# Order of the weight and key/value transfers on SyncE in a fused retention and gated-MLP kernel

## Chip, cores and metric

The kernel runs on one core of one Trainium2 chip. The metric is the device time of one execution in microseconds (us); the figure for a kernel is the median of its runs.

## What is computed

The first half is a retention layer: per batch (4) and head (8), a 64x64 state decays by a fixed factor per head and gains an outer product of key and value at each of 768 positions; the query reads it. The second half is a two-layer network with an elementwise gate on the 3072 resulting rows of 512 numbers.

```python
for t in range(S):
    state = gamma[None, :, None, None] * state + np.einsum('bhd,bhe->bhde', k[:, :, t], v[:, :, t])
    y[:, :, t] = scale * np.einsum('bhd,bhde->bhe', q[:, :, t], state)
...
h = x @ w_in                      # 3072x512 by 512x2048
sp = np.maximum(h, 0.0) + np.log1p(np.exp(-np.abs(h)))
g = h * erf(sp)
return (g @ w_out).astype(np.float32)   # 3072x2048 by 2048x512
```

The weights `w_in` and `w_out` arrive as 64-bit numbers and are turned into 32-bit ones on the chip.

## The kernel before

**Tiling.** The 3072 rows are cut into 24 chunks of 128 positions and 12 groups of 256 rows (two chunks a group). The hidden width of 2048 is cut into 8 pieces of 256. Weight pieces are numbered 0 to 7 for `w_in` and 8 to 15 for `w_out`; a raw piece of `w_out` is 1 MB of 64-bit words in one of four buffers of the pool `wide`.

**Stages.** The first four chunks (groups 0 and 1) go through a start-up stage. Then the loop at L881 runs over groups 2 to 11, each in eight slots `i`. A slot emits `unit` (L598), the first product for one of the 8 hidden pieces: 24 matmuls on TensorE (L608), three terms of operands that are split into high and low parts. Its `put` (L625) joins the terms on ScalarE (L256) and VectorE (L257) and has GpSimd store the piece of hidden values to a scratch area (L631). When all groups are done, the hidden values are read back, gated and multiplied by `w_out` (L792).

**Retention inside the loop.** While group g multiplies, the two chunks 2g+2 and 2g+3 of the next group are computed between its units. `begin` (L483; scores L489, state updates L496) runs ahead of unit 2 in groups 4 to 9 (ahead of unit 3 in group 2, 2 in group 3); `results` (L518) ahead of unit 5. `begin` needs the values scaled by L473.

**Loads for the group after.** In group g, `load_pair(2g+4)` (L113) fetches the chunks that `begin` uses in group g+1. It is a generator that yields after every four transfers: eight batches of four 32 KB transfers for keys and queries in blocks (`kb`, `qb`, L122), then one last batch with keys and values of both chunks, 256 KB each, in the order kn, v, kn, v (L131, L111). I call these 36 transfers a pair. `steps(pair, 2)` at L889 advances the generator by two batches in each slot, so kn and v come in slot 4. `prepare` (L457) scales the queries and transposes the blocks in slot 7, and scales the values (L473) in slot 0 of the next group.

**Conversion of w_out.** `conversion` (L165) turns a raw piece into 32-bit numbers in five steps: L181 with L182 on ScalarE; L185; L189; L192, after which the raw buffer is free; L203. `convert` advances it by 1, 2, 1, 1 and 2 steps in slots 0 to 4 of groups 4 to 9, seven a group, in the lists that `beside` (L825) returns. So piece 8 starts in slot 0 of group 4, piece 14 in slot 1 of group 8 and piece 15 in slot 0 of group 9.

**Where raw pieces are asked for.** Piece 8 in slot 4 of group 2; pieces 9, 10 and 11 in slots 1, 3 and 5 of group 3; pieces 12 to 15 inside `conversion`, behind L192 of the piece four before (L197, L198), which falls in groups 4, 5, 5 and 6. All these transfers, and those of a pair, are issued by SyncE (queue SP).

**What sets the order.** The schedule is written by hand: each engine executes its instructions in the order in which the Python code emits them. A tile's buffer comes from its pool in the order in which buffers were given back, and the first writer waits for the last reader of the tile before. For SyncE the program also lets each transfer wait until the one eight issues earlier has landed, so eight at most are under way, and an instruction that waits holds back all behind it.

Of the kernel before, what the change touches and what calls it, by code (L numbers as in the profile page):

```python
# [40 lines left out]
def kernel(  # L41
# [22 lines left out]
    NPC = n_ft // 2  # L64
# [14 lines left out]
    def b4(name, shape, dtype=F32):  # L79
        return big.tile([P] + shape, dtype, name=name, tag="b4")  # L80
# [19 lines left out]
    def load(j):  # L100

        kq = b4("kq", [2, H, D])
        KN[j], QN[j] = kq[:, 0], kq[:, 1]
        for to, src in ((KN[j], k), (QN[j], q)):
            nc.sync.dma_start(to, of_chunk(src, j))

    def load_values(j):
        if j % 2 == 0:
            VP[j] = b4("v", [2, H, D])
        V[j] = VP[j - j % 2][:, j % 2]  # L110
        nc.sync.dma_start(V[j], of_chunk(v, j))  # L111
# [32 lines left out]
    def load_piece(n, *parts):  # L144

        if n not in RAW:
            RAW[n] = b8("raw", [2 * d_model], I64)
        if n < NPC:
            rows = (slice(2), slice(2, 4)) if n == 0 else (slice(4),)
            for part, g, r in itertools.product(parts or (None,), rows, range(2)):  # L150
                f = slice(2 * P) if part is None else slice(part * P, (part + 1) * P)
                nc.sync.dma_start(
                    RAW[n][r * D : (r + 1) * D].rearrange("p (g f) -> p g f", g=n_k)[:, g, f],
                    w_in[r * DH : (r + 1) * DH, n * 2 * P : (n + 1) * 2 * P].rearrange(
                        "(g p) f -> p g f", p=D
                    )[:, g, f],
                )
        else:
            i = n - NPC
            nc.sync.dma_start(  # L160
                RAW[n].rearrange("p (f c) -> p f c", f=2),
                w_out[i * 2 * P : (i + 1) * 2 * P, :].rearrange("(f p) c -> p f c", p=P),
            )

    def conversion(n):  # L165

        WF[n] = b4("w", [2, 2, 2 * P])
        POWER[n] = b4("power", [2, 2, 2 * P])  # L170
        parts = itertools.product(
            range(2) if n < 4 else (None,), (slice(1), slice(1, 2)) if n == 0 else (slice(None),)
        )
        for part, rows in parts:
            last = n > 0 or rows.start == 1
            f = slice(2 * P) if part is None else slice(part * P, (part + 1) * P)
            words = RAW[n].bitcast(U32).rearrange("p (h a b w) -> p h a b w", h=2, a=2, w=2)[:, rows, :, f]
            to, power = WF[n][:, rows, :, f], POWER[n][:, rows, :, f].bitcast(U32)
            number = to.bitcast(U32)
            lo, hi = words[..., 0], words[..., 1]  # L180
            nc.vector.tensor_scalar(power, hi, 0x7FF00000, None, op0=ALU.bitwise_and)  # L181
            nc.scalar.activation(power, power, AF.Relu, bias=below, scale=8.0)  # L182
            if part is None:
                yield
            nc.vector.tensor_scalar(  # L185
                number, hi, 0xFFFFF, 1 << 20, op0=ALU.bitwise_and, op1=ALU.bitwise_or
            )
            yield
            nc.vector.scalar_tensor_tensor(to, number, 2.0**32, lo, op0=ALU.mult, op1=ALU.add)  # L189
            if part is None:  # L190
                yield
            nc.vector.scalar_tensor_tensor(  # L192
                power, hi, 1 << 31, power, op0=ALU.bitwise_and, op1=ALU.bitwise_or
            )
            if part != 0 and last:
                del RAW[n]
                if n + 4 < NPC or n >= NPC and n + 4 < 2 * NPC:  # L197
                    load_piece(n + 4)  # L198
                if n < 2:
                    load(JPC + n)  # L200
                    load_values(JPC + n)
            yield
            nc.vector.scalar_tensor_tensor(  # L203
                to, to, 2.0**-52, power.bitcast(F32), op0=ALU.mult, op1=ALU.mult,
            )
            if last and n < NPC:
                done.update(("in", 2 * n + u) for u in (range(2) if part is None else (part,)))
            yield
        if n >= NPC:
            nc.gpsimd.dma_start(  # L210
                WOF[n - NPC], WF.pop(n).rearrange("p h a f -> p (h a f)").rearrange("p (f c) -> p f c", f=2)
            )
# [472 lines left out]
    def steps(s, n=1):  # L685
        for _ in range(n):
            next(s, None)

    pair = load_pair(JPC + 2)
    prep = prepare(JPC + 2)  # L690
    a, b = JPC, JPC + 1
# [120 lines left out]
    def on_pe(g):  # L812

        a, b = 2 * g + 2, 2 * g + 3
        if a >= NJ:
            return {}
        if g < NG - 2:
            m = 3 if g == G2 else 2
            return {
                m: [(begin, a, ps_h), (begin, b, ps_r)],  # L820
                5: [(results, a, None, ps_h), (results, b, None, ps_r)],
            }
        return {1: [(begin, a)], 2: [(results, a)], 3: [(begin, b)], 5: [(results, b)]}

    def beside(g, prep, next_prep):  # L825

        a, b = 2 * g + 2, 2 * g + 3
        if g == G2:
            return {
                1: [(split_weights, 4)],  # L830
                2: [(split_weights, 5)],
                3: [(states, a), (states, b)],
                4: [(split_weights, 6), (load_piece, 8)],
                5: [(crossed_sums, a), (split_x, a)],
                6: [(crossed_sums, b), (split_x, b)],
                7: [(steps, next_prep, 3)],
            }
        if g == G2 + 1:
            return {
                0: [(steps, prep)],  # L840
                1: [(split_weights, 7), (load_piece, 9)],
                2: [(states, a)],
                3: [(states, b), (load_piece, 10)],
                5: [(crossed_sums, a), (split_x, a), (load_piece, 11)],
                6: [(crossed_sums, b), (split_x, b)],
                7: [(steps, next_prep, 3)],
            }
        if g < NG - 2:
            return {
                0: [(steps, prep), (convert, 1)],  # L850
                1: [(convert, 2)],
                2: [(states, a), (convert, 1)],
                3: [(states, b), (convert, 1)],
                4: [(convert, 2)],
                5: [(crossed_sums, a), (split_x, a)],
                6: [(crossed_sums, b), (split_x, b)],
                7: [(steps, next_prep, 3)],
            }
        if g == NG - 2:
            return {  # L860
                0: [(steps, prep), (load_w_out, 0)],
                1: [(states, a), (load_w_out, 1)],
                2: [(crossed_sums, a), (split_w_out, 0), (load_hiddens, 0)],
                3: [(states, b), (split_x, a)],
                4: [(split_w_out, 1), (softplus, 0)],
                5: [(erf, 0), (crossed_sums, b), (load_w_out, 2)],
                6: [(split_x, b), (gated, 0), (load_hiddens, 1)],
                7: [(split_w_out, 2), (split_g, 0)],
            }
        return {  # L870
            0: [(split_g, 1), (softplus, 1), (load_w_out, 3)],
            1: [(erf, 1), (load_w_out, 4)],
            2: [(split_w_out, 3), (load_w_out, 5)],
            3: [(gated, 1), (split_w_out, 4)],
            4: [(split_g, 2), (load_w_out, 6), (load_hiddens, 2)],
            5: [(split_w_out, 5), (load_w_out, 7)],
            6: [(split_g, 3)],
            7: [(split_w_out, 6)],
        }

    for g in range(G2, NG):  # L881
        pair = load_pair(2 * g + 4) if 2 * g + 4 < NJ else iter(())
        next_prep = prepare(2 * g + 4) if 2 * g + 4 < NJ else iter(())
        pe, other = on_pe(g), beside(g, prep, next_prep)
        for i, n in enumerate((0, 7, 1, 2, 3, 4, 5, 6) if g == G2 else range(NPC)):
            for f, *args in pe.get(i, ()):
                f(*args)
            put = unit(g, n)
            steps(pair, 2)  # L889
            if g == NG - 1:  # L890
                W.pop(n)
            for f, *args in other.get(i, ()):
                f(*args)
            put()
        prep = next_prep
    split_w_out(7)

    for n in range(NG * NU):
        g, i = divmod(n, NU)
# [62 lines left out]
```

## Time and profile before

| what | value |
|---|---|
| runs | 641.16, 638.66 and 639.08 us, median 639.08 |
| profiled execution | 644.27 us, of which the span from first to last instruction is 642.6 us |
| TensorE matmul (PE) busy | 624.8 us, 97% of the span |
| VectorE (DVE) busy | 473.7 us, 74% |
| ScalarE (ACT) busy | 346.5 us, 54% |
| GpSimd (POOL) busy | 81.6 us, 13% |
| SyncE's queue of transfers (q1) | 75.92 MB, 48.8% of 16 DMA engines |
| GpSimd's queue (q0) | 29.38 MB, 12.6% |
| mean granted TensorE clock | 0.986 of full speed |

The profile is of one execution. Times in its rows are microseconds from the first instruction, except where ns is written. PE is the matmul stream of TensorE, DVE is VectorE, ACT ScalarE, POOL GpSimd, and SPq is SyncE's instruction stream, where a row's length is the time that issuing took, waits included. A row of the waits names who waited, for whom, the total in us, how often and the longest. L numbers are lines of the kernel before.

### The profile page before, as it was taken

What the parts mean: (1) busy time and instruction counts of PE and PEld (TensorE: products, weight loads), DVE (VectorE), ACT (ScalarE), POOL (GpSimd) and SP (SyncE); (2) the same over time, 40 slices, a digit from 0 to 9 for tenths busy, and PEclk for the clock granted to TensorE, in tenths of its full rate; (3) what the DMA queues carried; (4) which work ended last, traced back from release to release, by engine and by line L of the source; (5) the groups of instructions that cost most, each with busy time, mean ns of one, the idle gap of its engine ahead of it and who ended that gap; (6) DMA issues with size and microseconds to landing.
All of it is one profiled execution on the core that took longest, in us unless ns stands there. A gap on an engine that the chain in (4) does not pass through costs nothing.

```text
span 642.6 us, 14651 instructions
## 1 busy us (share of the span) xinstructions
PE 624.8 (97%) x6080; PEld 562.2 (87%) x6080; DVE 473.7 (74%) x618; ACT 346.5 (54%) x432; POOL 81.6 (13%) x157
## 2 busy tenths in 40 slices
PE   8999999997989997999999999999999999999997
PEld 7788899997989997999999988888888888888886
DVE  4988998754767876787776998776867686777650
ACT  3333443231413231323237877988898889888920
POOL 1054421110211211122111110000000000000000
PEclk9999999997989997999999999999999999999999
DMA  9999776878778986768865662534253325323300
GB/s 190 218 210 240 207 176 154 223 204 225 217 158 223 258 229 157 199 173 207 213 206 166 204 239 82 165 110 137 83 163 132 88 108 163 132 78 120 99 33 33
DMA packets 165042, 106.36 MB, mean 166 GB/s; under 512 B 139248, under 2 KB 143600, under 8 KB 164976
## 3 DMA queue, kind: packets, MB, share of 16 engines
q1 hardware_dynamic: 154784, 75.92, 48.8%
q0 software_dynamic: 9632, 29.38, 12.6%
q8 instruction: 47, 0.77, 0.5%
q10 hardware_dynamic: 560, 0.14, 0.1%
q14 instruction: 19, 0.16, 0.1%
HBM read 69.75 MB, written 35.65 MB: 164 GB/s over the span
## 4 chain that ended last, share of the span: by engine, by line
PE 61%; DMA 1%; SPq 1%; DVE 1%; issue 0%; ACT 0%; DVEq 0%
PE o L792 20%; PE o L608 16%; PE hp L792 10%; PE r L792 10%; DMA v<-in_v_dram 1%; PE hp L608 1%; PE r L608 1%; SPq L131 1%; PE hp L496 0%; PE r L534 0%; PE hp L489 0%; PE r L545 0%; PE r L489 0%; PE r L496 0%; PE hp L534 0%
## 5 line engine op out<-in xcount | busy, mean ns | idle before, releaser
L608 PE MATMUL o<-x_hi,w_hi 128*128 128x256 f32 x600 | 152.6, 291 | 0.0
L608 PE MATMUL o<-x_lo,w_lo 128*128 128x256 f32 x600 | 149.7, 286 | 0.0
L608 PEld LDWEIGHTS o<-x_hi,w_hi 128*128 128x128 f32 x600 | 117.4, 196 | 1.6
L608 PEld LDWEIGHTS o<-x_lo,w_lo 128*128 128x128 f32 x600 | 117.4, 196 | 0.1
L256 ACT ACTIVATE h<-o 128x512 f32<-128x512 f32 x75 | 44.2, 593 | 104.5 <-PE o L608 103.7
L747 DVE TENSOR_TENSOR e<-hid,e 128x1024 f32<-128x1024 f32 x48 | 56.7, 1222 | 58.2 <-ACT e L737 58.2
L608 PE MATMUL o<-x_dif,w_dif 128*128 128x256 f32 x600 | 84.1, 283 | 0.0
L608 PEld LDWEIGHTS o<-x_dif,w_dif 128*128 128x128 f32 x600 | 77.4, 192 | 0.0
L631 POOL DMA_DIRECT2D hid<-h x80 | 44.2, 552 | 243.6 <-DVE h L257 237.8
L792 PE MATMUL o<-w_dif,g_dif 128*128 128x512 f32 x192 | 73.7, 389 | 0.0
L257 DVE SCALAR_TENSOR_TENSOR h<-o,h 128x512 f32<-128x512 f32 x75 | 51.2, 683 | 29.8 <-ACT h L256 19.2
L792 PE MATMUL o<-w_hi,g_hi 128*128 128x512 f32 x168 | 65.4, 389 | 0.0
L792 PE MATMUL o<-w_lo,g_lo 128*128 128x512 f32 x168 | 65.4, 389 | 0.0
L250 DVE SCALAR_TENSOR_TENSOR g_dif<-g_hi,g_lo 128x1024 fp32r<-128x1024 f32 x48 | 58.8, 1225 | 3.2
L248 ACT ACTIVATE g_hi<-e 128x1024 fp32r<-128x1024 f32 x48 | 51.0, 1062 | 17.8 <-DVE e L747 15.1
L249 DVE TENSOR_TENSOR g_lo<-e,g_hi 128x1024 fp32r<-128x1024 f32 x48 | 58.6, 1222 | 0.2
L583 PE MATMUL hp<-xT,w 128*128 128x256 f32 x256 | 57.2, 382 | 1.4 <-ACT xT L447 1.3
L583 PEld LDWEIGHTS hp<-xT,w 128*128 128x128 f32 x256 | 48.0, 190 | 8.6 <-ACT xT L447 1.5
L182 ACT ACTIVATE power<-power,below 128x1024 uint32<-128x1024 uint32 (+2 forms) x22 | 20.2, 920 | 54.9 <-DVE power L181 52.4
L737 ACT ACTIVATE e<-e 128x1024 f32<-128x1024 f32 x48 | 48.2, 1053 | 0.3
L733 ACT ACTIVATE e<-hid 128x1024 f32<-128x1024 f32 x48 | 48.2, 1052 | 0.3
L792 PEld LDWEIGHTS o<-w_dif,g_dif 128*128 128x128 f32 x192 | 36.0, 188 | 7.4
(164 smaller groups left out, 1078.3 us busy)
## 6 DMA issues: line engine op xcount, KB each, us to landing
hid<-hid SPq DMA_DIRECT2D x48, 512.0 KB, 4.7
hid<-h POOLq DMA_DIRECT2D x80, 256.0 KB, 3.4
raw<-in_moe_w_out_dram SPq DMA_DIRECT2D x8, 1024.0 KB, 7.4
v<-in_v_dram SPq DMA_DIRECT2D x24, 256.0 KB, 5.4
out_dram<-y SPq DMA_DIRECT2D x23, 256.0 KB, 2.1
kb<-in_k_dram SPq DMA_DIRECT2D x144, 32.0 KB, 2.9
qb<-in_q_dram SPq DMA_DIRECT2D x144, 32.0 KB, 2.7
kn<-in_k_dram SPq DMA_DIRECT2D x18, 256.0 KB, 5.0
```

Source lines behind the costliest of these rows:

```text
L248: nc.scalar.activation(hi, x, AF.Copy, scale=KEEP)
L249: nc.vector.tensor_tensor(lo, x, hi.bitcast(F32), op=ALU.subtract)
L250: nc.vector.scalar_tensor_tensor(dif, hi.bitcast(F32), Z, lo.bitcast(F32), op0=ALU.mult, op1=ALU.subtract)
L256: nc.scalar.activation(to, a, AF.Copy, scale=1 + 1 / Z)
L257: nc.vector.scalar_tensor_tensor(to, b, -1 / Z, to, op0=ALU.mult, op1=ALU.add)
L583: nc.tensor.matmul(HP_[ft][:, g], w[:, kk, ft % 2 * P : (ft % 2 + 1) * P], XC[g][:, kk], start=(kk == 0), stop=(kk == n_k - 1),)
L608: nc.tensor.matmul(to[:, u], W[n][i][:, kk * 2 * P + u * P : kk * 2 * P + (u + 1) * P], X[g][i][:, kk], start=(u == 0 and kk == 0 and i == ...
L631: nc.gpsimd.dma_start(HID[g][:, 2 * n : 2 * n + 2], h)
L733: nc.scalar.activation(E[n], HID_[n], AF.Softplus)
L737: nc.scalar.activation(E[n], E[n], AF.Erf)
L747: nc.vector.tensor_tensor(E[n], HID_.pop(n), E[n], op=ALU.mult)
L792: nc.tensor.matmul(Y[g][t][x // 2], G[n][x][:, f, t * P : (t + 1) * P], W_OUT[ft // 2][x][:, ft % 2 * d_model : (ft % 2 + 1) * d_model], s ...
```

## The change

Three things change.

1. `conversion` no longer asks for a piece of `w_out`; only the pieces of `w_in` are still asked for there.
2. `beside` asks for the pieces instead: 9 and 10 in slots 3 and 5 of group 3 (9, 10 and 11 in slots 1, 3 and 5 before), and then one a group, piece g+7 in slot 3 of groups 4 to 8. The request stands behind the slot's `convert`.
3. `steps(pair, 3)` advances the pair by three batches a slot, so the batch with kn and v comes in slot 2, ahead of the request for the raw piece in slot 3.

```diff
             if part != 0 and last:
                 del RAW[n]
-                if n + 4 < NPC or n >= NPC and n + 4 < 2 * NPC:
+                if n + 4 < NPC:
                     load_piece(n + 4)
...
         if g == G2 + 1:
             return {
                 0: [(steps, prep)],
-                1: [(split_weights, 7), (load_piece, 9)],
+                1: [(split_weights, 7)],
                 2: [(states, a)],
-                3: [(states, b), (load_piece, 10)],
-                5: [(crossed_sums, a), (split_x, a), (load_piece, 11)],
+                3: [(states, b), (load_piece, 9)],
+                5: [(crossed_sums, a), (split_x, a), (load_piece, 10)],
...
-                3: [(states, b), (convert, 1)],
+                3: [(states, b), (convert, 1)] + [(load_piece, g + 7)] * (g + 7 < 2 * NPC),
...
             put = unit(g, n)
-            steps(pair, 2)
+            steps(pair, 3)
```

## Prediction

> **What bounds the kernel now.** First the slices of the page: TensorE is busy nearly everywhere, and its granted clock dips in slices 9, 11 and 15 (about 145 to 257 us).
>
> ```profile
> PE   8999999997989997999999999999999999999997
> PEclk9999999997989997999999999999999999999999
> ```
>
> Then the waits of the engines, for what TensorE lacks there.
>
> ```profile
> DVE v L473 <- DMA v<-in_v_dram: 15.9, 4, 6.5
> PE hp L496 <- DVE v L473: 9.6, 3, 4.0
> ```
>
> TensorE waits three times for the scaled values, VectorE four times for the values to land; TensorE has no other wait over 1.5 us. Then the chain of work that ended last shows how the third stall came about.
>
> ```profile
> 235.08 4.32 SPq L131
> 239.44 6.27 DMA v<-in_v_dram
> 245.80 1.24 DVE v L473
> 247.08 1.13 PE hp L496 x32
> ```
>
> SyncE was late in issuing kn and v; the values landed at 245.71, and TensorE went on 1.4 us after that. Last, the starts of the first `begin` matmul of groups 3 to 10 give the price, in the timeline of TensorE.
>
> ```profile
> 122.84 0.69 PE L489 MATMUL hp<-qT,kT 64*64 64x64 f32 x32
> 150.30 0.69 PE L489 MATMUL hp<-qT,kT 64*64 64x64 f32 x32
> 154.96 1.13 PE L496 MATMUL hp<-v,kn 64*64 64x64 f32 x32 [3.96 <-DVE v L473]
> 184.36 0.69 PE L489 MATMUL hp<-qT,kT 64*64 64x64 f32 x32
> 187.12 0.69 PE L496 MATMUL hp<-v,kn 64*64 64x64 f32 x32 [2.07 <-DVE v L473]
> 215.38 0.69 PE L489 MATMUL hp<-qT,kT 64*64 64x64 f32 x32
> 242.84 0.69 PE L489 MATMUL hp<-qT,kT 64*64 64x64 f32 x32
> 247.08 1.13 PE L496 MATMUL hp<-v,kn 64*64 64x64 f32 x32 [3.54 <-DVE v L473]
> 276.49 0.69 PE L489 MATMUL hp<-qT,kT 64*64 64x64 f32 x32
> 303.72 0.69 PE L489 MATMUL hp<-qT,kT 64*64 64x64 f32 x32
> 328.31 0.69 PE L489 MATMUL hp<-qT,kT 64*64 64x64 f32 x32
> ```
>
> An undisturbed group takes 27.46 us (122.84 to 150.30, 215.38 to 242.84) or 27.23 (276.49 to 303.72; groups 5 and 8, whose first chunk opens a batch). The disturbed ones take 34.06, 31.02 and 33.65, so they lose 6.60, 3.79 and 6.19: **16.6 us** together. The idle time is only 9.6 of that. The rest is clock: after a stall the matmuls run slower for some microseconds.
>
> ```profile
> 150.00:160.00 10.00, 6.04 (x126) 5.65 (x125) 4.52 (x6) 2.12 (x3) 0.54 (x1) 0.68 0.85 211
> 180.00:190.00 10.00, 7.93 (x168) 7.54 (x168) 7.07 (x9) 1.19 (x2) 1.08 (x2) 0.89 0.79 160
> ```
>
> In these stretches of the busy times (PE, PEld, DVE, ACT, POOL, then clock, DMA share, GB/s) the clock is 0.68 and 0.89. The Trainium skill ("TensorE: Matmul & The Clock Gate", section "Part 1: The HAM clock gate") has the clock halve after an idle window of about 3.4 us. The stalls of 3.96 and 3.54 agree; the one of 2.07 us lost 3.79, more than the rule lets it.
>
> **Why SyncE is late.** Its timeline from group 2 on: the first block transfers of each pair (kb), some of the raw pieces, and the last v of the pair that began at 241.01.
>
> ```profile
> 88.62 2.80 SPq L122 DMA_DIRECT2D kb<-in_k_dram  x4
> 112.55 1.08 SPq L160 DMA_DIRECT2D raw<-in_moe_w_out_dram  x1
> 113.73 2.82 SPq L122 DMA_DIRECT2D kb<-in_k_dram  x4
> 127.16 0.45 SPq L160 DMA_DIRECT2D raw<-in_moe_w_out_dram  x1
> 140.80 0.46 SPq L160 DMA_DIRECT2D raw<-in_moe_w_out_dram  x1
> 151.42 2.63 SPq L122 DMA_DIRECT2D kb<-in_k_dram  x4
> 182.49 2.56 SPq L122 DMA_DIRECT2D kb<-in_k_dram  x4
> 211.18 2.94 SPq L122 DMA_DIRECT2D kb<-in_k_dram  x4
> 233.50 0.40 SPq L160 DMA_DIRECT2D raw<-in_moe_w_out_dram  x1
> 241.01 4.00 SPq L122 DMA_DIRECT2D kb<-in_k_dram  x4
> 264.53 1.37 SPq L111 DMA_DIRECT2D v<-in_v_dram  x1
> 269.75 1.88 SPq L122 DMA_DIRECT2D kb<-in_k_dram  x4
> 290.96 4.33 SPq L122 DMA_DIRECT2D kb<-in_k_dram  x4
> ```
>
> A pair without raw pieces takes 23.9 us (88.62 to 112.55) or 21.2 (269.75 to 290.96). The four pairs from 113.73 to 241.01 take 127.28, with pieces 9 to 15 among them and the tail of piece 8. With a pair at 23.9 that is (127.28 - 95.6)/8 = 4.0 us for a raw piece, and 27.9 us for a pair with one piece; with 21.2 it is 5.3 and 26.5. Before, seven pieces stand ahead of the values of pair 16, the last that stall; so SyncE falls behind, although a pair with one piece would about fit a group of 27.4.
>
> **The change, part by part.**
>
> *Raw pieces.* No transfer is added or dropped. Pieces 9 and 10 go behind the values of pair 10, pieces 11 to 15 behind those of pairs 12 to 20. Ahead of pair 16's values stand only 9 to 12, three pieces fewer, 12 to 16 us of SyncE's time by the two prices: about what was lost by then.
>
> *Three batches a slot.* By itself this moves nothing: SyncE has its next instructions queued and works at transfers. It only sees to it that kn and v are emitted ahead of slot 3's piece. Two slots earlier kn and v take buffers given back at the last group's end, at nearly the same place in the order, so I cost that at 0. SyncE does wait for buffers:
>
> ```profile
> SPq L122 <- DMA raw<-in_moe_w_out_dram: 11.0, 5, 2.9
> SPq L122 <- PE o L608: 9.0, 6, 3.9
> ```
>
> The second row is buffers that TensorE frees; it keeps SyncE from running more than a few microseconds ahead of the groups, so no lead can be saved up. The first is issues held up by a raw piece in flight, part of the 4.0.
>
> *What is late next.* I follow SyncE through the changed order, with undisturbed groups: `begin` would start at 150.30, 177.76, 204.99, 232.45, 259.91, 287.14 and 311.73 (groups 4 to 10). The values must land 0.85 earlier (1.4 for scaling and start, less 0.5 of L489 matmuls that come first). Landing times come from the transfers' rows:
>
> ```profile
> DMA to landing us min/median/max: 4.0/5.6/9.0
> DMA to landing us min/median/max: 6.0/7.4/9.2
> ```
>
> The first is for the values, the second for the raw pieces, both in the loop. The last v is issued about 1 us before its pair's end, so it lands 4.6 behind that end.
>
> With 23.9 and 4.0: pair 10 ends at 113.73 + 27.9 = 141.6, values at 146.2 (limit 149.4: the first stall is gone). Pair 12 has two pieces ahead: 173.5, values 178.1, 1.2 late. From there one cycle of 27.9 a group: pair 14 is 1.9 late, 20 is 3.4, and 22, whose `begin` comes a slot earlier, lands at 317.6 against 310.9, 6.7 late. With 21.2 and 5.3 the cycle is 26.5 and nothing is late: the residue is 0. If half of the 9.0 us of buffer waits fell into the stretch of 127.28 (my estimate; there are four of the seven pairs in it), the transfers took less: a piece 3.4, the cycle 27.3, the residue 2. With the slowest pair, 24.9 from 241.01 to the end of its last issue, the cycle is 28.4 and the residue 9.4. I take 4, between 2 and 6.7, and keep 0 and 9.4 as the ends.
>
> *The new wait.* Piece 15 was issued at 233.50 and used 68 us later; now it is issued behind pair 20's values, just ahead of group 9, where L181 reads it.
>
> ```profile
> 301.27 0.68 DVE L181 TENSOR_SCALAR power<-raw 128x1024 uint32<-128x1024 uint32 x1
> 303.66 0.69 DVE L257 SCALAR_TENSOR_TENSOR h<-o,h 128x512 f32<-128x512 f32 x1 [1.70 <-ACT h L256]
> ```
>
> L181 starts 2.45 before group 9's `begin`. Behind it on VectorE wait the joining of unit 0 (L257), on ScalarE L182 and L256, and unit 2 on TensorE needs L257's bank free: about 1.5 us of slack. So the piece must land by 287.14 - 2.45 + 1.5 = 286.2. Issued at 141.6 + 31.9 + 4 x 27.9 = 285.1 it lands at 292.5, 6.3 late; at a cycle of 27.3, about 2; at 26.5, not late. It overlaps with the lateness of the values, which is the same SyncE, so it adds nothing to the residue of 4. Piece 14 has two slots more.
>
> *Sum.* Each stall cost 1.7 to 2.6 beyond its idle time; small ones should cost less, so I add 1 to the residue for the clock: 5. Gain 16.6 - 5 = 11.6. The profiled execution took 644.27, 1.67 beyond its span: 632.7. The median of the runs is 5.2 below the profiled one. If that is a fixed cost of profiling, the forecast is 639.08 - 11.6 = 627.5; if the profiled run merely stalled more, about 11.4 is to be had in the others, and with a small residue the result is about the same. I take **627.5**. By the skill's rule, stalls under 3.4 us leave the clock alone, which gives 626.5. Another rule speaks against the change: "DMA: Bandwidth & Descriptors" (section "Anatomy of one DMA", a fit for GpSimd's transfers) makes a 1 MB transfer 4.4 us, an estimate; then the cycle is 28.3 and the result about 633.
>
> **The rivals.** With a raw piece at 4.0, the residue follows from the cycle c: 113.73 + 7c + 4.0 + 4.6 - 310.9 = 7c - 188.6.
>
> *Little is gained.* Transfers stay the bound: the same bytes pass the same queue. For it speaks that 182.49 to 211.18, a pair with piece 13 and with 14 just issued, took 28.7; at that cycle the residue is 12.3, 13.3 with the clock, and the result 635.8. At 29.2 nothing is gained: 639. Against it: part of those 28.7 was waiting, and one and a bit pieces were in it. Nor would anything be gained if the unprofiled runs hardly stalled; but then they would be 11.4 us slower than the profiled one outside the stalls (644.27 - 16.6 = 627.7).
>
> *Slower.* With TensorE unstalled, GpSimd's stores come closer together and slow SyncE's queue. Then the values land late in every group, and in groups 8 and 9 the raw piece later still, so that L181 holds up VectorE. The price is seven cycles: at c = 30 the residue is 21.4, 22.4 with the clock, and the result 645. It decides from 29.6 on (slower by over 0.5%). For it: the pair from 151.42 to 182.49 took 31.1. Against it: two pieces fell into that, and no pair with one took as long.
>
> *The change does nothing.* If the stalls came from GpSimd's stores and not from the raw pieces, the order would not matter. The pairs of 21.2 and 23.9 with those stores beside them speak against it; it falls in with the first rival.
>
> **How the numbers follow.** Forecast (residue 0 to 11.4, clock included; 622.5 to 634): 0.70. A smaller gain (634 to 635.9): 0.08. Within 0.5%, about what a measurement of this kernel can tell from no change (635.9 to 642.3): 0.11. Slower: 0.11. So faster 0.78, same 0.11, slower 0.11. The range from 622 to 636 holds the first two cases and a little more.
>
> **What would show it.** Right: L496 no longer waits for L473, or under 2 us at a time; groups of 27.5; clock 9 in slices 9, 11 and 15; raw pieces on SyncE behind v; the same PE busy time. The new wait would show as VectorE at L181 waiting for raw in groups 8 and 9. Wrong: SyncE's cycle over 29 us with one piece, or stalls that move to groups 8 to 10.

## The result and the profile after

| kernel | median of the runs | lowest to highest | profiled execution, span |
|---|---|---|---|
| before | 639.52 us (6 runs) | 638.66 to 641.74 | 644.27, 642.6 (not one of the 6) |
| changed | 632.65 us (6 runs) | 629.71 to 634.94 | 632.97, 631.3 |

The ratio is 0.9884, interval 0.9853 to 0.9914: faster by 6.9 us in the medians. The forecast was 627.5, with a range of 622 to 636. Two later runs, 646.66 us of the kernel before and 644.64 us of one experiment, count as slow, over 1.5% above the fastest run of their kernel, and the ratios and the ranges given below leave them out.

The page's slices of the changed kernel: the dips in the clock are gone, and TensorE has only a shallow one in slice 11.

```profile
PE   8999999999989999999999999999999999999997
PEclk9999999999999999999999999999999999999999
```

The waits of the engines: VectorE waits 5.6 us for the values in place of 15.9, and a new row stands below it, L181 waiting for a raw piece. TensorE's wait at L496 has gone from 9.6 to 1.4, but it now waits 3.2 for the bank that ScalarE and VectorE empty: once in group 5 behind the late values (0.9), and twice, in groups 8 and 9, behind the late L181 (0.8 and 1.5).

```profile
DVE v L473 <- DMA v<-in_v_dram: 5.6, 4, 2.5
DVE power L181 <- DMA raw<-in_moe_w_out_dram: 2.8, 2, 2.6
PE hp L496 <- DVE v L473: 1.4, 2, 1.0
PE o L608 <- ACT h L256: 3.2, 3, 1.5
```

The first `begin` matmuls of groups 3 to 10 in TensorE's timeline:

```profile
122.43 0.69 PE L489 MATMUL hp<-qT,kT 64*64 64x64 f32 x32
149.90 0.69 PE L489 MATMUL hp<-qT,kT 64*64 64x64 f32 x32
177.35 0.69 PE L489 MATMUL hp<-qT,kT 64*64 64x64 f32 x32
206.96 0.69 PE L489 MATMUL hp<-qT,kT 64*64 64x64 f32 x32
234.43 0.69 PE L489 MATMUL hp<-qT,kT 64*64 64x64 f32 x32
261.89 0.69 PE L489 MATMUL hp<-qT,kT 64*64 64x64 f32 x32
290.38 0.69 PE L489 MATMUL hp<-qT,kT 64*64 64x64 f32 x32
316.52 0.69 PE L489 MATMUL hp<-qT,kT 64*64 64x64 f32 x32
```

The groups take 27.47, 27.45, 29.61, 27.47, 27.46, 28.49 and 26.14 us; undisturbed they would take 27.46, 27.46, 27.23, 27.46, 27.46, 27.23 and 24.59, by the trace of before. So 2.4 us are lost in group 5, 1.3 in group 8 and 1.6 in group 9, together 5.2 in place of 16.6. SyncE's timeline shows the new order, and how long a pair with a piece takes (first kb of pairs 10, 12, 20 and 22, and pieces 9 and 10, 14 and 15):

```profile
113.13 2.12 SPq L122 DMA_DIRECT2D kb<-in_k_dram  x4
141.07 1.36 SPq L160 DMA_DIRECT2D raw<-in_moe_w_out_dram  x2
142.54 2.72 SPq L122 DMA_DIRECT2D kb<-in_k_dram  x4
256.52 1.72 SPq L160 DMA_DIRECT2D raw<-in_moe_w_out_dram  x1
258.42 2.91 SPq L122 DMA_DIRECT2D kb<-in_k_dram  x4
282.24 1.17 SPq L111 DMA_DIRECT2D v<-in_v_dram  x1
283.45 1.59 SPq L160 DMA_DIRECT2D raw<-in_moe_w_out_dram  x1
285.15 2.60 SPq L122 DMA_DIRECT2D kb<-in_k_dram  x4
```

Each piece now stands right behind the last v. The six pairs from 113.13 to 285.15, with seven pieces among them (8 to 14), take 28.7 us on average, longer than a group. So SyncE is late still, only less so. What VectorE waited for, in its timeline:

```profile
177.80 1.22 DVE L473 TENSOR_TENSOR v<-v,kq_s 128x1024 f32<-128x1024 f32 x1 [2.50 <-DMA v<-in_v_dram]
232.61 1.23 DVE L473 TENSOR_TENSOR v<-v,kq_s 128x1024 f32<-128x1024 f32 x1 [1.69 <-DMA v<-in_v_dram]
261.27 1.22 DVE L473 TENSOR_TENSOR v<-v,kq_s 128x1024 f32<-128x1024 f32 x1 [1.07 <-DMA v<-in_v_dram]
265.63 0.69 DVE L181 TENSOR_SCALAR power<-raw 128x1024 uint32<-128x1024 uint32 x1 [0.27 <-DMA raw<-in_moe_w_out_dram]
291.55 0.69 DVE L181 TENSOR_SCALAR power<-raw 128x1024 uint32<-128x1024 uint32 x1 [2.57 <-DMA raw<-in_moe_w_out_dram]
316.28 1.23 DVE L473 TENSOR_TENSOR v<-v,kq_s 128x1024 f32<-128x1024 f32 x1 [0.38 <-DMA v<-in_v_dram]
```

Pair 10 (wanted in group 4) is on time; pair 12, with two pieces ahead of it, is the first that is late; pieces 14 and 15 are late for their conversion.

### The profile page after: what moved, and what is told of

Read it like the earlier page. It is cut to its first block, busy times and chain, and to the rows that moved or that the text cites. A ratio compares the mean times of both kernels' runs of the same rounds, so it can differ in the third digit from the quotient of the medians.

```text
span 631.3 us, 14653 instructions
## 1 busy us (share of the span) xinstructions
PE 618.3 (98%) x6080; PEld 555.8 (88%) x6080; DVE 473.1 (75%) x618; ACT 346.4 (55%) x432; POOL 81.3 (13%) x157
## 4 chain that ended last, share of the span: by engine, by line
PE 84%; DMA 5%; issue 4%; DVE 4%; SPq 1%; ACT 1%; POOL 1%; DVEq 0%; ACTq 0%; POOLq 0%
PE o L608 25%; PE o L792 21%; PE hp L792 10%; PE r L792 10%; PE hp L583 9%; DMA raw<-in_moe_w_out_dram 1%; DMA kb<-in_k_dram 1%; DMA v<-in_v_dram 1%; DMA hid<-h 1%; PE hp L608 1%; PE r L608 1%; DMA kq<-in_q_dram 1%; PE r L534 1%; PE hp L489 1%; PE r L545 1%
## 5 line engine op out<-in xcount | busy, mean ns | idle before, releaser
L608 PE MATMUL o<-x_hi,w_hi 128*128 128x256 f32 x600 | 149.7, 287 | 3.2 <-ACT h L256 3.2
L608 PE MATMUL o<-x_lo,w_lo 128*128 128x256 f32 x600 | 147.1, 283 | 0.0
L608 PEld LDWEIGHTS o<-x_hi,w_hi 128*128 128x128 f32 x600 | 114.9, 192 | 5.1 <-ACT h L256 3.7
L608 PEld LDWEIGHTS o<-x_lo,w_lo 128*128 128x128 f32 x600 | 115.0, 192 | 0.1
L608 PE MATMUL o<-x_dif,w_dif 128*128 128x256 f32 x600 | 84.1, 283 | 0.0
L608 PEld LDWEIGHTS o<-x_dif,w_dif 128*128 128x128 f32 x600 | 77.4, 192 | 0.0
L249 DVE TENSOR_TENSOR g_lo<-e,g_hi 128x1024 fp32r<-128x1024 f32 x48 | 58.6, 1221 | 0.2
```

The source lines that it names most:

```text
L249: nc.vector.tensor_tensor(lo, x, hi.bitcast(F32), op=ALU.subtract)
L608: nc.tensor.matmul(to[:, u], W[n][i][:, kk * 2 * P + u * P : kk * 2 * P + (u + 1) * P], X[g][i][:, kk], start=(u == 0 and kk == 0 and i == ...
```

## The experiments

The theory is that the megabytes of raw pieces on SyncE's queue ahead of a pair's values make them late, at some 3.9 us a piece. The rivals are that handing the pair over earlier is what helps, that only an even spread counts, that GpSimd's stores or the block transfers are to blame, and that the DMA engines, not SyncE's queue, are what a piece takes. The kernels below were measured in three sets, the first four of the table, the next four and the last three; kernels of a set (a "call" in the recorded expectations) share their runs of the kernel before. Between sets, and with the result above, ratios are compared.

| kernel | median, us | ratio to before (interval) |
|---|---|---|
| batches only | 635.46 | 0.9889 (0.9840 to 0.9939) |
| pieces only | 638.67 | 0.9951 (0.9920 to 0.9983) |
| pieces 9 to 15 not loaded | 627.39 | 0.9766 (0.9716 to 0.9816) |
| pieces on GpSimd's queue | 631.48 | 0.9839 (0.9789 to 0.9889) |
| changed, second set | 634.35 | 0.9870 (0.9839 to 0.9900) |
| every piece a group later | 639.66 | 0.9941 (0.9908 to 0.9975) |
| piece 15 used later | 634.43 | 0.9877 (0.9847 to 0.9907) |
| a group later, on GpSimd's queue | 636.09 | 0.9903 (0.9871 to 0.9935) |
| changed, third set | 633.11 | 0.9888 (0.9840 to 0.9935) |
| pieces on GpSimd's queue, again | 628.97 | 0.9826 (0.9785 to 0.9868) |
| the same, evenly spread | 631.14 | 0.9853 (0.9810 to 0.9897) |

**Pieces 9 to 15 not loaded.**

```diff
+    first_raw = []
...
     def load_piece(n, *parts):
...
+        if n > NPC:
+            RAW[n] = first_raw[0]
+            return
...
             i = n - NPC
+            first_raw.append(RAW[n])
```

> The changed kernel with raw pieces 9 to 15 not loaded: their conversions read piece 8 again, so half of w_out is replaced and 7 MB of transfers are left out. Theory (the raw pieces are all that makes SyncE late): no wait of VectorE for values or raw pieces, groups of 27.2 to 27.5 us, 627 to 628 us, ratio about 0.982, span about 626. Rival (GpSimd's stores or the block transfers make it late too): waits at L473 stay and the time stays at or above 630, ratio 0.985 or more.

Measured: 627.39 us, in six runs from 627.05 to 627.78, span 625.6. (Seven of the eight pieces of `w_out` are replaced, not half of it.) No row of VectorE or TensorE waiting for the loop's values is left, and the groups take 27.46, 27.46, 27.24, 27.46, 27.46, 27.24 and 24.58 us. This is the floor for this loop, and it is steady from run to run, while the kernel before spread from 636.6 to 646.1 in that set. So the raw pieces are what makes the stalls, shown by taking them out; the kernel before loses some 12 to 14 us to them, the changed one 5 to 7. GpSimd's stores and the block transfers alone do no harm.

**Batches only**: the kernel before with three batches a slot.

```diff
-            steps(pair, 2)
+            steps(pair, 3)
```

> The kernel before with three batches a slot, raw pieces asked for where they were. Theory (what counts is how many raw pieces stand on SyncE ahead of each pair's values, some 3.9 us each): ahead of the values of pairs 12, 14, 16 and 18 now stand 3, 5, 6 and 7 pieces behind piece 8 (before 4, 5, 7, 7; in the changed kernel 2, 3, 4, 5), so the last stalls are some 4 us shorter than before and 5 to 7 longer than in the changed kernel: 636 us, ratio to before 0.990 to 1.000. Rival (handing the pair over earlier is itself what helps): as fast as the changed kernel, ratio about 0.989 or below.

Measured: 635.46 us, 6.1 below the kernel before of its set. In microseconds that is what the count of pieces had, 636; but the ratio, 0.9889, is the rival's 0.989 and just outside the theory's 0.990 to 1.000, so the run doesn't part the two. The profiled waits are smaller than before and longer than in the changed kernel:

```profile
DVE v L473 <- DMA v<-in_v_dram: 8.9, 4, 2.9
PE hp L496 <- DVE v L473: 2.0, 2, 1.8
```

What follows is that this one number brings most of the gain, and by the ratio all of it (0.9889 against 0.9870 to 0.9888 for the changed kernel). What it changes in the order is seen in its trace: pieces 10, 12 and 15, issued ahead of a pair's kn and v before (at 140.80, 167.33 and 233.50 us), now stand behind them (143.96, 175.06 and 232.70). That the gain comes from this and from nothing else in the earlier hand-over isn't shown.

**Pieces only**: the changed kernel with two batches a slot.

```diff
-            steps(pair, 3)
+            steps(pair, 2)
```

> The changed kernel with two batches a slot, so that the raw piece of slot 3 stands ahead of the keys and values of slot 4. Theory (pieces ahead of the values count): one piece more ahead of every pair's values than in the changed kernel, 3.9 us later, while pieces 14 and 15 come earlier: residue about 6 to 8 in place of 5, 634 to 636 us, ratio 0.991 to 0.996. Rival (only the even spread over the groups counts, not the order inside a group): the same as the changed kernel, 0.989.

Measured: 638.67 us, only 2.9 below the kernel before of its set. The sign of the theory holds, and the rival of the even spread falls (0.9951 with an interval that begins at 0.9920, against 0.9884 and an interval that ends at 0.9914). The ratio lies in the theory's range, but the size in microseconds was missed: 11 us above the floor and not 6 to 8. A reading that fits, and that no run tests by itself: a piece right ahead of kn and v costs more than one further back, since the values then also take longer to land. The two landing rows of v in the loop, of this kernel and then of the changed one:

```profile
DMA to landing us min/median/max: 5.0/7.2/10.0
```

```profile
DMA to landing us min/median/max: 4.0/5.2/6.8
```

**Pieces on GpSimd's queue**, at the same places of the program.

```diff
             i = n - NPC
-            nc.sync.dma_start(
+            nc.gpsimd.dma_start(
```

> The changed kernel with the raw pieces of w_out issued by GpSimd in place of SyncE, at the same places of the program. Theory (a piece delays the pairs because it stands in SyncE's queue ahead of them): SyncE's cycle falls to about 24, the waits at L473 go, 628 us, ratio about 0.982. Rival (the DMA engines' bandwidth is what a piece takes, whichever queue it comes from): SyncE's cycle stays near 28 and the time near 632, ratio 0.989.

Measured: 631.48 us, nearer to the rival's 632 than to the theory's 628, while the ratio (0.9839) is nearer to the theory's. SyncE's first kb of pairs 10 and 22:

```profile
115.01 3.18 SPq L122 DMA_DIRECT2D kb<-in_k_dram  x4
282.97 2.56 SPq L122 DMA_DIRECT2D kb<-in_k_dram  x4
```

Six pairs take 28.0 us each although no piece is in SyncE's queue, and not the 24 that the theory gave. But SyncE also waits for buffers there, so the pace alone doesn't say what a piece takes. The kernel without pieces is the measure for that. Its first kb of the same pairs, and the two largest rows of what SyncE waited for from 113 to 286 (total, times, longest; line numbers of this kernel are 6 higher, so L255 is L249 and L614 is L608):

```profile
113.04 3.40 SPq L122 DMA_DIRECT2D kb<-in_k_dram  x4
274.05 3.79 SPq L122 DMA_DIRECT2D kb<-in_k_dram  x4
```

```profile
SPq L122 <- DVE x_lo L255: 11.7, 3, 5.0
SPq L122 <- PE o L614: 4.6, 10, 1.3
```

The same waits of the kernel with the pieces on GpSimd's queue, and of the changed one:

```profile
SPq L122 <- PE o L608: 3.6, 6, 1.1
SPq L111 <- DVE x_dif L250: 2.6, 1, 2.6
```

```profile
SPq L122 <- PE o L608: 5.4, 5, 3.7
SPq L131 <- PE o L608: 1.2, 2, 0.9
```

With the smaller rows, and without the one wait of 1.3 us that falls behind 274.05, the waits for TensorE and VectorE come to 15.9, 8.8 and 7.1 us. Without them the six pairs take 161.0 - 15.9 = 145.1 with no piece behind 8 (24.2 a pair), 168.0 - 8.8 = 159.2 with seven on GpSimd's queue, and 172.0 - 7.1 = 164.9 with seven on SyncE's. That makes an estimate of 2.0 us a piece there, and 2.8 here (3.3 without piece 15, which is issued only 1.7 us before the end). So by SyncE's pace a piece takes time that the pairs need whichever queue it comes from, and some 1 us more on SyncE's own.

TensorE's loss says more for the queue. No L181 waits for a piece any more, and VectorE's waits for values, 5.2 us in all against 5.6, hardly reach TensorE: behind group 3 the groups take 27.46, 27.24, 27.46, 27.78, 27.59 and 25.01 us, 1.1 over the undisturbed ones. (Group 3 itself loses 0.9, in the stall of the last section.) The changed kernel loses 5.2 above, and 6.5 and 4.1 in its two other profiles below. The next two measure it again, beside the changed kernel.

> The changed kernel as the measure for the two others of this call: ratio to before 0.986 to 0.991, some 5 to 7 us above the 627.4 us without pieces 9 to 15.

> The changed kernel with the pieces of w_out on GpSimd's queue, once more. If what a piece takes is the DMA engines' time alone: within 1 us of the changed kernel of this call. If SyncE's queue counts as well: 2 to 3 us below it, as the earlier two calls had it (631.5 against 632.7 and 634.4 us).

Measured: 633.11 and 628.97 us (ratios 0.9888 and 0.9826, with intervals that overlap between 0.9840 and 0.9868). The second is 4.1 below the first, more than the 2 to 3 of the reading on record by which SyncE's queue counts as well, and well beyond the 1 us of the other. Its groups behind group 3 are undisturbed (27.47, 27.23, 27.46, 27.46, 27.24 and 24.58 us); the whole loss of its profiled execution, 3.9 us, lies in group 3, in the stall of the last section, which also gives SyncE that much time to catch up. It is the fastest kernel here that does all the work, and clear of the kernel before, but not shown to be faster than the changed one beyond the intervals.

**Pieces on GpSimd's queue, evenly spread.**

```diff
-                5: [(crossed_sums, a), (split_x, a), (load_piece, 10)],
+                5: [(crossed_sums, a), (split_x, a)],
...
-                3: [(states, b), (convert, 1)] + [(load_piece, g + 7)] * (g + 7 < 2 * NPC),
+                3: [(states, b), (convert, 1)],
...
+    AT = {(4, 2): 10, (5, 1): 11, (6, 0): 12, (6, 6): 13, (7, 5): 14, (8, 3): 15}
...
+            if (g, i) in AT:
+                load_piece(AT[g, i])
```

> The pieces on GpSimd's queue and evenly spread, one every 54 or so units of a sixth of a group: piece 9 in slot 3 of group 3, then 10 to 15 in group 4 slot 2, 5 slot 1, 6 slot 0, 6 slot 6, 7 slot 5 and 8 slot 3, conversions as in the changed kernel. Theory (bytes ahead of a pair's values count): without the two pieces in group 3 the first 1.3 us of lateness go, 629 to 630.5 us. Rival (the engines' time over the whole loop counts, not its spread): the same as the kernel before in this call, 631 to 632.

Measured: 631.14 us, no better than the uneven spread (628.97), with intervals that overlap. The gain that the theory expected isn't there; but there was little left to gain. In the profiles of both kernels TensorE waits for values by 0.2 us at most, and what they lose in the loop is nearly all in stalls of the kind of the last section.

**Every piece behind 9 a group later**, and the changed kernel beside it.

```diff
-                5: [(crossed_sums, a), (split_x, a), (load_piece, 10)],
+                5: [(crossed_sums, a), (split_x, a)],
...
-                0: [(steps, prep), (convert, 1)],
-                1: [(convert, 2)],
-                2: [(states, a), (convert, 1)],
-                3: [(states, b), (convert, 1)] + [(load_piece, g + 7)] * (g + 7 < 2 * NPC),
+                0: [(steps, prep)] + [(convert, 2)] * (g == G2 + 2),
+                1: [(convert, 2)] * (g == G2 + 2),
+                2: [(states, a)] + [(convert, 1)] * (g == G2 + 2),
+                3: [(states, b), (convert, 1), (load_piece, g + 6)],
                 4: [(convert, 2)],
-                5: [(crossed_sums, a), (split_x, a)],
-                6: [(crossed_sums, b), (split_x, b)],
+                5: [(crossed_sums, a), (split_x, a), (convert, 1)],
+                6: [(crossed_sums, b), (split_x, b), (convert, 1)],
```

Group 10 gets the same five conversion steps in its slots 3 to 6, and a converted piece is stored with its last step.

> The changed kernel once more, as the measure for the others of this call. Both theories: ratio to before 0.986 to 0.991, about 5 us above the 627.4 us of the kernel without pieces 9 to 15.

> The changed kernel with every piece behind 9 one group later (10 in group 4 up to 15 in group 9, one a group, no pair of pieces in group 3), each converted in slots 3 to 6 of the group after, so that the last two end in group 10. Theory (bytes ahead of the values count, 3.9 us a piece): one piece less ahead of the values of pairs 12 to 22, only pair 22 is still late by some 1.6 us, residue 2, 629 to 630 us, 2.5 to 4 us below the changed kernel of this call. Rival (a cycle of SyncE is longer than a group with one piece whatever the start): lateness still grows group by group and the gain is under 1 us; or the conversions moved into group 10 take the gain back.

Measured: 634.35 for the changed kernel and 639.66 here, so the gain that I expected turned into a loss. First and last kb of the six pairs in SyncE's timeline, and TensorE's longest stall in its own:

```profile
113.03 2.72 SPq L122 DMA_DIRECT2D kb<-in_k_dram  x4
288.01 2.31 SPq L122 DMA_DIRECT2D kb<-in_k_dram  x4
```

```profile
322.40 1.14 PE L496 MATMUL hp<-v,kn 64*64 64x64 f32 x32 [4.16 <-DVE v L473]
```

29.2 us a pair with one piece each: in this execution the rival's case, lateness that grows until the last pair. But it took 644.64, the longest of the twelve and 5 us above the median, so whether the others show it is not known. Six pieces fall into these pairs, and seven into those of the changed kernel; why the six cost more stays open. The second part of the rival is seen more cleanly in the next run.

**A group later, on GpSimd's queue**: both edits.

> The kernel with pieces one group later, and these issued by GpSimd. Theory after the run of the changed kernel on GpSimd's queue (what a piece takes is the DMA engines' time, not SyncE's place): as the one on SyncE, within 1.5 us, 628 to 630 us. Rival (the queue counts as well): 1.5 us or more below it, down to the 627.4 us without the pieces.

Measured: 636.09 us, 3.6 below the run on SyncE's queue, so here too the reading on record by which the queue counts as well. But it is over 4 above the pieces on GpSimd's queue at the changed kernel's places (631.48 and 628.97, other sets), and far from the 628 to 630 foreseen. In the loop little is late: the second `begin` of group 10 starts at 322.50, against 325.40 in the changed kernel and 319.77 in the one without pieces.

```profile
322.50 0.69 PE L489 MATMUL hp<-qT,kT 64*64 64x64 f32 x32
```

```profile
325.40 0.69 PE L489 MATMUL hp<-qT,kT 64*64 64x64 f32 x32
```

The time is lost behind it. From that matmul to the end of the span it is 634.1 - 322.5 = 311.6 us, and 631.3 - 325.4 = 305.9 in the changed kernel (305.8 in the kernel without pieces). The run before, which has conversions in group 10 too, takes 642.9 - 332.1 = 310.8. So, as far as two profiles show it, the conversions put into group 10 cost 5 to 5.7 us, which would make up the loss of the run before as well (5.3 in the medians).

**Piece 15 used later**: in group 9 conversion starts in slot 2.

```diff
+        if g == NG - 3:
+            return {
+                0: [(steps, prep)],
+                2: [(states, a), (convert, 1)],
+                3: [(states, b), (convert, 1)],
+                4: [(convert, 2)],
+                5: [(crossed_sums, a), (split_x, a), (convert, 1)],
+                6: [(crossed_sums, b), (split_x, b), (convert, 1)],
+                7: [(steps, next_prep, 3)],
+            }
```

> The changed kernel with the conversion of piece 15 begun in slot 2 of group 9 and not in slot 0. Theory (the wait of L181 for piece 15 costs 1.5 us of its own in group 9): 1 to 1.5 us below the changed kernel of this call. Rival (it is the same lateness of SyncE that pair 22 shows one group later): the wait of L181 goes, the wait at L473 for pair 22 grows by as much, no difference.

Measured: 634.43 against 634.35: the rival. In VectorE's timeline, the last two rows of waiting of the changed kernel in this set, and of this one:

```profile
293.08 0.70 DVE L181 TENSOR_SCALAR power<-raw 128x1024 uint32<-128x1024 uint32 x1 [2.98 <-DMA raw<-in_moe_w_out_dram]
317.67 1.23 DVE L473 TENSOR_TENSOR v<-v,kq_s 128x1024 f32<-128x1024 f32 x1 [0.23 <-DMA v<-in_v_dram]
```

```profile
291.44 0.69 DVE L181 TENSOR_SCALAR power<-raw 128x1024 uint32<-128x1024 uint32 x1 [0.16 <-DMA raw<-in_moe_w_out_dram]
316.34 1.22 DVE L473 TENSOR_TENSOR v<-v,kq_s 128x1024 f32<-128x1024 f32 x1 [2.48 <-DMA v<-in_v_dram]
```

The wait of 2.98 for the piece became 0.16, and that of 0.23 for the values became 2.48. It is one lateness, and whoever asks first pays.

## Why the prediction was right, and where it was off

**What bounds the kernel** was right, and shown: without the pieces the loop has no stall for values, and its groups' lengths came out within 0.01 us of the undisturbed ones that were read off the trace of before.

**The sum** for the profiled execution was 11.6 us of gain; the span went from 642.6 to 631.3, 11.3. The residue, taken as 5 with the clock, is 5.2 by the group lengths.

**The step that failed is the one from the profiled execution to the median.** It subtracted the 5.2 us between them as "a fixed cost of profiling". Profiling costs nothing of the kind: of the twelve times that a kernel was measured after the prediction, the profiled execution lies among the other runs of its kernel in eight (the changed one: 632.97, the others 629.71 to 634.94), below them in two and above them in two. The kernel before scatters by 9.5 us, 636.6 to 646.1 in the set of the floor, while the floor scatters by 0.7; so the profiled execution had merely stalled more. That was the other reading the text gave, and with the residue of 5 it makes 627.4 + 5 = 632.4 for a measured 632.65. Instead I let the two readings give "about the same", by leaving the residue out of the second. The measured time lies in the range, but 5.2 above the number that I took.

**The price of a piece.** By the text's own count, with one piece extra, the cycle is (172.0 - 4.0)/6 = 28.0 us, against 27.9. Pair 22's values, foreseen at 317.6, were taken up by VectorE at 316.28. The residue was less sure than that: the text's formula gives 6.7 at 27.9 and 7.4 at 28.0, and the 4 was a choice between two prices, so that 4 and 1 for the clock met 5.2 is luck in part. Without SyncE's waits for buffers a piece costs about 3, not 4.0, and of what was argued as SyncE's queue time some 2.0 are also taken from GpSimd's queue; both are the estimates worked out above. The rule from the Trainium skill that the prediction set against the change ("DMA: Bandwidth & Descriptors", "Anatomy of one DMA", an estimate of 4.4 us a piece and about 633 us) came near the median by another way: the piece is cheaper here than that, and the rest came from the step above.

**"By itself this moves nothing"** was wrong for the batches. That part alone brought 6.1 us, and its trace has kn and v ahead of three pieces asked for in the old places. I had weighed it only together with the new place in slot 3. So the part that was costed at 0 brings most of the gain, and the new places, which the sum went by, only 2.9 us alone.

**The new wait** at L181 for pieces 14 and 15 came as foreseen, 0.27 and 2.57 us, and using piece 15 later confirmed that it adds nothing to the lateness of the values.

**The clock.** The stalls left in the changed kernel are 1.5 us and less, and the granted clock is 0.999. These stalls agree with the rule that the prediction named from the Trainium skill ("TensorE: Matmul & The Clock Gate", "Part 1: The HAM clock gate"), by which the clock is halved after an idle window of some 3.4 us; the 2.07 us of the kernel before do not. In these traces the length of a stall doesn't decide alone: after 2.28 us (pieces on GpSimd's queue, again) the clock was 0.83 over 139 to 149 us, after 2.85 us (pieces only) 0.66 over 268 to 278, and after 3.31 us (changed, third set) 1.00 over 290 to 300. I had added 1 us for the clock; TensorE's waits at L496 and L608, 1.4 and 3.2 us, are 4.6 of the 5.2 lost, so 0.6 is left for it and all else.

**The rivals.** "Little is gained" had the right mechanism (bytes, not their order) in part: it is why 5 to 7 us of the 12 to 14 remain. "Slower" didn't come: it decides from a cycle of 29.6 on, and the cycle is 28.0.

## What to carry to other kernels

Where an engine waits for a transfer, count the bytes that the program issued ahead of it since the last time the issuing queue had nothing to do, and move what is needed later behind it; here a one-number change of the hand-over did most of that. Measure each part of a change alone, also one costed at 0. A transfer moved to another queue isn't free: here the pairs still took 28.0 us each, though TensorE lost less. Before a gain from one profiled execution is carried over to the median, look at the scatter of the runs: here the stalls that hang on transfers differed from run to run, and the floor hardly did.

## What the runs showed that was not expected

In five of the profiles TensorE stalled once in group 3 without any releaser. The row with the pieces on GpSimd's queue, measured again:

```profile
139.94 0.28 PE L608 MATMUL o<-x_hi,w_hi 128*128 128x256 f32 x1 [2.28 <-issue]
```

It is 2.28 us there and in the kernel with batches only, 2.61 in the evenly spread one, 0.79 in the first run on GpSimd's queue, 0.95 in the one a group later on that queue, and absent in the changed kernel. In each a raw piece was in flight at that time. After it the matmuls of the row shown ran at 0.41 us each and not 0.28 for some 3 us, and group 3 took 31.36 us in place of 27.46.

The timing in the traces points at the loads of instructions (queue q8, 16 KB each). In these five profiles one such load ends at 136.6 to 138.6 us, and TensorE goes on 1.3 to 1.5 us after that end in each. In the eight others the same load ends by 135.8, and there is no stall. Three shorter stalls without a releaser later in the loop (0.67 to 0.76 us) end 1.4 to 1.5 us behind such a load too. Why the load comes late in the five stays open, and no run was made to test it.
